# A loan of 384 columns, earlier exchanges and turns, and transfers paced by TensorE's columns

## The chip, the cores and the metric

The kernel runs on one core of a Trainium2 chip (trn2). The metric is the time of one execution on the device in microseconds (us), as the median of several runs. A core has TensorE (PE in the profile; its weight loads are PEld), VectorE (DVE), ScalarE (ACT), GpSimd (POOL) and SyncE (SP), each with its own queue of instructions, and 16 DMA engines that move data for all queues. Here almost all transfers are issued by SP.

## What is computed

Attention with a threshold over 8 batches and 8 heads of 576 rows and 64 columns, then a bilinear feed-forward layer on the heads side by side (4608 tokens of 512 numbers, 1536 inner columns), all in 32-bit floats:

```python
def _attn_ref(q, k, v, tau):
    scale = 1.0 / np.sqrt(q.shape[-1])
    scores = scale * np.matmul(q, k.transpose(0, 1, 3, 2))
    thresh = np.max(scores, axis=-1, keepdims=True) - tau
    scores = np.where(scores >= thresh, scores, -1000000000.0)
    scores = scores - np.max(scores, axis=-1, keepdims=True)
    attn = np.exp(scores)
    attn = attn / (np.sum(attn, axis=-1, keepdims=True) + 1e-09)
    return np.matmul(attn, v).astype(np.float32)

def _moe_ref(x, w_a, w_b, w_out):
    a = x @ w_a
    b = x @ w_b
    return (a * b @ w_out).astype(np.float32)
```

Between the two, `attn_out.transpose(0, 2, 1, 3)` brings the heads of a token side by side.

## The kernel before

**Units and slots.** The heads are taken in 32 pairs (`pairs`), the rows of a pair in five units: four of 128 rows and one of 64 (`NT`). The outer loop goes over 160 units; one turn of it (`g`) is a slot, and each slot works on several units at once, each at another stage:

- `scores(g)`: TensorE computes the scores of unit g into two PSUM tiles (L352), DVE takes the row maxima (L359) and the threshold (L360).
- `weigh(g)`: ACT takes the exponential (L380), DVE masks it and sums the rows (L383); then the reciprocal of the sums (L394, L396) and `normalise` on ACT (L402).
- `turn_blocks(g-1)`: DVE transposes the weights in blocks of 32 x 32 (L446), and SP writes them in four transfers to a buffer in memory, `swap` (L457).
- `turn_back(g-2)`: SP reads them from there in turned order into a tile `wT` (L466, 576 KB in one transfer; L469 for the unit of 64 rows). There are two tiles `wT`.
- `weighted(g-3)` (`PV_LAG` is 3): where a half of a pair is complete, TensorE multiplies the turned weights with v (L483, a *product*, of 128 columns, or 160 where the unit of 64 rows goes with it), and `settle` copies the result to x: one copy on ACT (L490), two on DVE (L491), and the same again into `xt` for the 32 columns of the unit of 64 rows.

The first eight units are turned by TensorE itself (`BY_PE`). In the first 30 or so slots the weights of the feed-forward layer are loaded as well, and ACT, POOL and DVE convert them.

**The feed-forward layer as filler.** When four pairs have filled a tile of x, `exchange_blocks` copies its two halves of partitions crosswise into a second tile, `xS` (POOL, eight copies, L506), makes two tiles of differences, `xU` (L513), and puts the block on a list. `ffn` is a generator that yields after every few matmuls: 128 columns a step in `sevens_of` (L633), 256 in `plain` (L706) and in the output layer (L763). A column here is one column of the moving operand in four matmuls that share TensorE's array. `advance(cols)` runs the generator until as many columns have been spent. Each slot has a budget of columns (`pace`), given out in four portions (`PORTIONS`: 0.3, 0.35, 0.15, 0.2): the first after `turn_blocks`, the second ahead of the product, the last two at the slot's end. The product's own columns are taken off the account (`running["owed"]`), so the last two portions of a slot with a product are mostly eaten by it.

**Buffers.** All results in PSUM go through four tiles of two banks each (`banks`). The tiles xT, xS, xU and xt share seven buffers (`XT_BUFS`); `make_x` runs the feed-forward layer ahead until a buffer is free. `kept` and `osb` are rows of the output that `store` sends out (L833).

**Order.** Each engine runs its instructions in the order in which the code emits them; `keep_order` fixes that. SP's queue in a slot is: swap writes of the unit before (they wait for L446), read back of the unit before that (it waits for the product that last used the `wT` tile), then loads of q, k (`load`, L147) and v (`load_v`, L170), then output. `prep` transposes a loaded q or k in place on DVE (L320). A transfer by SP uses one of eight semaphores in turn, so it waits for the eighth transfer before it.

**Start.** q and k of the first pairs come as rows (`load_rows`), TensorE transposes them (`prep_pe`, L333) and DVE copies the result (`prep_copy`, L338). Six small operations on DVE (L305 to L310) derive five numbers from `tau`, which SP loads (L290) after the first rows.

Of the kernel before, what the change touches and what calls it, by code (L numbers as in the profile page):

```python
# [14 lines left out]
ALU = mybir.AluOpType  # L15
# [7 lines left out]
PV_LAG = 3  # L23
BY_PE = 8
# [4 lines left out]
CATCH_UP = 0.05  # L29
PACE_EARLY = 0.04  # L30
ROOM = 1024
PORTIONS = (0.3, 0.35, 0.15, 0.2)
RAWS = 4
TW_BUFS = 3
# [18 lines left out]
def kernel(  # L53
# [41 lines left out]
    Q = 32  # L95
# [24 lines left out]
    loads = pool("loads", 3)  # L120
    work = pool("work", 2)
    small = pool("small", 2)
    scratch = pool("scratch", 3, space=bass.MemoryType.DRAM)
    psum = pool("psum", 4, space=PSUM)

    def banks(n, name):
# [5 lines left out]
    NPR = len(pairs)  # L132
    loaded = {}

    def load(i, name, engine=nc.sync):

        b, hp = pairs[i]
        src = {"q": q, "k": k}[name[0]]
        n0, n1 = {"k": (0, NB), "q0": (0, HALF // Q), "q1": (HALF // Q, NB)}[name]
        bufs = HP if name == "k" else Q_BUFS  # L140
        most = NB if name == "k" else NB - HALF // Q
        t = work.tile([P, most, Q], FP32, tag=name[0] + "T", bufs=bufs, name=name[0] + "T")[:, 0:n1 - n0]
        for j in range(2):
            rows = src[b, 2 * hp + j].rearrange("(e n) d -> e n d" if name == "k" else "(n e) d -> e n d", e=Q)
            for h in range(2):
                r = slice((2 * j + h) * Q, (2 * j + h + 1) * Q)
                engine.dma_start(t[r], rows[:, n0:n1, h * Q:(h + 1) * Q])  # L147
        loaded.setdefault(i, {})[name] = t

    def load_rows(i, name, room, engine=nc.sync):  # L150
# [7 lines left out]
    def load_v(i, again=False):  # L158
        b, hp = pairs[i]
        if not again:  # L160
            loaded[i]["v"] = loads.tile([P, NSLOT, D], FP32, tag="vm", bufs=HP, name="vm")
        for j in range(2):
            rows, half = v[b, 2 * hp + j], loaded[i]["v"][j * D:(j + 1) * D]
            if i >= HP or again:
                if i < HP:
                    rows = rows.rearrange("(c s p) d -> p c s d", c=2, p=Q)
                else:
                    rows = rows.rearrange("(p c s) d -> p c s d", c=2, p=Q)
                for c in range(2):
                    nc.sync.dma_start(half[c * Q:(c + 1) * Q], rows[:, c])  # L170
            else:
                nc.sync.dma_start(half, rows.rearrange("(s p) d -> p s d", p=D))

# [20 lines left out]
    for F in range(NF):  # L194
# [1 line left out]
    NPIECES = len(pieces)  # L196
    raws, stages, extra, taken = {}, {}, [], {}
    state = {"loaded": 0, "added": 0, "converted": 0, "rows": 0, "sums": False, "through": 0, "over": False,
             "layer": False, "reading": False, "first": 0}


    NSUM = NF // 2 * 3 * CH
# [82 lines left out]
    rooms = [t.rearrange("p (n w) -> p n w", n=NR) for t in rooms]  # L285
    load_rows(0, "q", rooms[0])
    load_rows(0, "k", rooms[1], nc.scalar)
    load_rows(1, "q", rooms[2])
    load_rows(1, "k", rooms[3], nc.scalar)
    nc.sync.dma_start(tau_sb, tau.to_broadcast([P, 1]))  # L290
    load_weights(2)
    load_rows(2, "q", rooms[4])
    load_rows(2, "k", rooms[5])
# [7 lines left out]

    ok, e_scale, e_nscale, cut, big = (scalars[:, c:c + 1] for c in range(5))
    nc.vector.tensor_scalar(ok, tau_sb, 0.0, None, op0=ALU.is_ge)  # L305
    nc.vector.tensor_scalar(e_scale, ok, SCALE, None, op0=ALU.mult)
    nc.vector.tensor_scalar(e_nscale, ok, -SCALE, None, op0=ALU.mult)
    nc.vector.tensor_scalar(big, ok, -BIG, BIG, op0=ALU.mult, op1=ALU.add)
    nc.vector.tensor_scalar(cut, tau_sb, 0.0, INV_SCALE, op0=ALU.max, op1=ALU.mult)
    nc.vector.tensor_tensor(cut, cut, big, op=ALU.add)  # L310


    prepared, scored, weights, turned, whole = {}, {}, {}, {}, {}
    x_of, xtail_of = {}, {}
    blocks, complete, swaps = [], [], {}

    def prep(i, name):

        mT = loaded[i].pop(name).rearrange("p n e -> p (n e)")
        nc.vector.transpose(mT, mT)  # L320
        prepared.setdefault(i, {})[name] = mT
# [119 lines left out]
    def turn_blocks(i, u):  # L441

        ws, _ = weights.pop((i, u))
        t = whole.pop((i, u))
        for w in ws:
            nc.vector.transpose(w, w)  # L446
        if u < NT:
            swap = scratch.tile([G, P, NSLOT * Q], FP32, tag="swap", name="swap")
        else:
            swap = scratch.tile([2, P, NSLOT * Q], FP32, tag="swapt", name="swap")  # L450
        swaps[i, u] = swap
        for g in range(G):
            if u < NT:
                to, n = swap[g], G
            else:
                to, n = swap[g % 2, (1 - g // 2) * D:(2 - g // 2) * D], 2
            nc.sync.dma_start(to.rearrange("(r p) e -> p r e", p=Q),  # L457
                              t[g * Q:(g + 1) * Q, 0:n * NSLOT].rearrange("p (r s) e -> p r (s e)", r=n))

    def turn_back(i, u):  # L460

        swap = swaps.pop((i, u)).rearrange("g p e -> p g e")
        if u < NT or i < HP:
            turned[i, u] = turned_tile()
            n = G if u < NT else 2
            nc.sync.dma_start(turned[i, u][:, 0:n].rearrange("p g s e -> p g (s e)"), swap)  # L466
        else:
            for y in range(2):
                nc.sync.dma_start(turned[i, 2 + y][:, G].rearrange("p s e -> p (s e)"), swap[:, y])  # L469

    def join(out, lo, hi):
        nc.scalar.copy(out, lo)
# [43 lines left out]
    def exchange_blocks():  # L516
        while complete and not state["layer"] and not blocks:
            x, what = complete.pop(0)
            xs = x_tile("xS")
            for hp in range(HP):  # L520
                exchange(x, xs, hp, 0, HALF, nc.gpsimd)
            blocks.append(((x, xs) + ((x_sums(x), x_sums(xs)) if state["first"] >= 3 * SEVENS else ()), what))

    def weighted_unit(i, u):

# [13 lines left out]
    def weighted(i, h):  # L539

        b, hp = pairs[i]
        n = width(i, h)
        if h < 2:
            groups = G + (n > HALF)
# [6 lines left out]
        if h < 2:  # L551
            if hp == 0:
                x_of[b, h] = x_tile("xT")
            settle(x_of[b, h][:, hp, :], pv, 0, P, read)
            if hp == HP - 1:
                complete.append((x_of.pop((b, h)), ("half", b, h)))
        if n % HALF:
            t = b % GT
# [271 lines left out]
    def store(n):  # L830

        for _ in range(n):
            nc.sync.dma_start(*pending.pop(0))  # L833

    BLOCK_COLS = NF * 2 * HP * HALF + 2 * NF * DM

# [1 line left out]

        return BLOCK_COLS - (NF // 2 * CH if state["sums"] else 0) - (SEVENS * 2 * HP * P if state["first"] >= 3 * SEVENS else 0)

    running = {"ffn": None, "owed": 0.0, "left": 0, "done": 0, "rest": 0, "room": 0}

    def advance(cols):
        running["owed"] += cols
        while running["owed"] > 0:
# [16 lines left out]
            if step is None:  # L862
                running["ffn"] = None
                state["through"] += 1
            else:
                running["owed"] -= step
                running["left"] -= step
                running["done"] = running["done"] + step if rest else 0
                running["rest"] = rest
                running["room"] = min(ROOM, whole // 2)  # L870
# [8 lines left out]

    def make_x(count):  # L880

        while (len([k for k in x_of if k != (0, 0)]) + len(xtail_of) + len(complete) + sum(len(x) for x, _ in blocks)
               + (state["reading"] and running["tiles"]) + count > XT_BUFS):
            owed = running["owed"]
            running["owed"] = 0.0
# [20 lines left out]
    first = {i: g for g, (i, u) in enumerate(units) if u == 0}  # L906
    second = {i: g for g, (i, u) in enumerate(units) if u == 2}

    for name in ("q", "k"):
        prep_copy(*prep_pe(0, name))  # L910
    early = {}

    def convert_rest(g, k):
# [10 lines left out]
        n += size  # L924
    for g in range(len(units) + PV_LAG):
        written = len(pending)
        state["converted"] = state["added"]
        here = g < len(units)
        converting = bool(early.get(g)) or bool(early.get(g - 1))
        if here:  # L930
            i, u = units[g]
            scores(i, u)
        exchange_blocks()
        pace = (PACE if g > BY_PE else PACE_EARLY) * BLOCK_COLS
        if g > BY_PE:
# [16 lines left out]
            turn_blocks(*units[g - 1])  # L952
        if g > BY_PE:
            advance(PORTIONS[0] * pace)
        if here:
            weigh(i, u)
        if here and g < BY_PE:
# [3 lines left out]
        if g < 3:  # L961
            prep_copy(*prep_pe(g + 1, "k"))
        for p in range(HP, NPR):
            for name, d in (("q0", 1), ("k", 2), ("q1", 1)):
                if g == (second if name == "q1" else first)[p] - d:
                    prep(p, name)
        if g > BY_PE:
            advance(PORTIONS[1] * pace)
            n = g - PV_LAG
            if BY_PE <= n < len(units) and part(*units[n]):  # L970
                p, h = part(*units[n])
                if pairs[p][1] == 0:
                    make_x(2 if h == 1 and p >= HP and pairs[p][0] % GT == 0 else 1)
                make_room()
                weighted(*part(*units[n]))
                running["owed"] -= NSLOT * width(*part(*units[n])) // 2
            if BY_PE + 1 < g <= len(units) + 1:
                turn_back(*units[g - 2])
        for n in early.get(g, [])[:1]:
            convert_first(n)  # L980
# [22 lines left out]
            load_v(g - BY_PE, again=True)  # L1003
        store(written)
        if g > BY_PE:
            advance(PORTIONS[2] * pace)
            advance(PORTIONS[3] * pace)

# [9 lines left out]
        if g > first[HP] + 1 and not converting and state["first"] < 3 * SEVENS:  # L1018
            first_sums(state["first"] % 3, state["first"] // 3)
            state["first"] += 1  # L1020
    state["over"] = True
    while complete or blocks or running["ffn"] is not None:
        advance(DM)
        store(len(pending))
# [33 lines left out]
```

## Time and profile before

| | |
|---|---|
| median of 8 runs | 1462.7 us (1459.64 to 1465.43) |
| the profiled execution, time | 1465.27 us |
| its span, first to last instruction | 1463.5 us |
| granted TensorE clock, mean | 0.993 |
| records of matmuls | 34208 |
| transfers in memory | 223.21 MB, mean 153 GB/s |

The page names groups of instructions by line, engine and the program's tiles. Its waits give the idle time of an engine just before an instruction and the instruction that ended it; "issue" stands for time for which the profile shows no cause. Of the groups that the change concerns:

| group | count | mean ns |
|---|---|---|
| L352 scores, 288 columns | 2016 + 288 records | 404, 441 |
| L483 products | 5184 records | 275 |
| L633 feed-forward, 128 columns | 14336 records | 270 |
| L446 transposes on DVE | 272 | 754 |
| L383 masking on DVE | 288 | 800 |
| L320 transposes of qT on DVE | 56 | 474 |
| L506 exchange on POOL | 152 | 400 (median) |

Records of TensorE overlap, four at a time and more, so that a mean is not the time that one takes of the span. Transfers, with size and median time from issue to landing: swap writes 480 of 144 KB, 2.6 us; wT reads 120 of 576 KB, 4.7 us, and 56 of 144 KB, 3.0 us; k 112 of 72 KB, 4.2 us; q 224 of 32 and 40 KB, 3.9 and 4.3 us; v 128 of 72 KB, 3.3 us; output 30 of 256 KB, 4.0 us.

### The profile page before, as it was taken

How to read it: one execution, taken by the hardware profiler on the slowest of the kernel's cores; microseconds unless marked ns; L12 is line 12 of the kernel's file. 1: busy time of each engine (PE TensorE's matmuls, PEld its weight loads, DVE VectorE, ACT ScalarE, POOL GpSimd, SP SyncE). 2: the span in 40 equal slices, each digit the busy share in tenths (PEclk: the TensorE clock that was granted, in tenths of full speed). 3: DMA queues.
4: the chain of work that ended last, by engine and by line, in shares of the span. 5: the costliest groups of instructions: out<-in, count | busy, mean ns of one | idle time of the engine just before them, and what ended most of it. 6: DMA issues, size and time to landing. Idle time of an engine off the chain costs nothing.

```text
span 1463.5 us, 76332 instructions
## 1 busy us (share of the span) xinstructions
PE 1390.3 (95%) x34208; PEld 1254.0 (86%) x34208; DVE 1014.5 (69%) x2245; ACT 684.5 (47%) x1243; POOL 480.9 (33%) x668
## 2 busy tenths in 40 slices
PE   5779999999999999999999999999999999999998
PEld 4678687888889989889998888888898879999998
DVE  6898688787767787586757677767867676655223
ACT  5786455545545554454444445444545455431110
POOL 2674723423060606033324224240606060605000
PEclk9999999999999999999999999999999999999999
DMA  9976677678756865576545766567756686550000
GB/s 208 227 209 181 162 180 185 169 175 194 192 134 161 186 182 148 143 174 179 144 131 135 169 168 165 129 170 163 183 146 152 160 194 160 127 150 31 4 18 17
DMA packets 325080, 223.21 MB, mean 153 GB/s; under 512 B 169616, under 2 KB 308880, under 8 KB 324752
## 3 DMA queue, kind: packets, MB, share of 16 engines
q1 hardware_dynamic: 322384, 217.73, 60.4%
q8 instruction: 269, 4.41, 1.3%
q10 hardware_dynamic: 2368, 0.59, 0.2%
q14 instruction: 59, 0.48, 0.1%
HBM read 128.58 MB, written 89.65 MB: 149 GB/s over the span
## 4 chain that ended last, share of the span: by engine, by line
PE 81%; DMA 6%; DVE 6%; SPq 3%; issue 3%; ACT 1%; POOL 1%; ACTq 0%; DVEq 0%; POOLq 0%
PE pab L633 26%; PE po L763 18%; PE pab L706 18%; PE pv L483 9%; PE sc L352 9%; DMA wT<-swap 1%; DVE mx L359 1%; DVE tw L446 1%; DMA raw<-in_moe_w_a_dram 1%; SPq L457 1%; DMA sums_u<-in_moe_w_a_dram 1%; PE po L809 1%; DVE tw L383 1%; DMA more_u<-in_moe_w_a_dram 1%; SPq L225 1%
## 5 line engine op out<-in xcount | busy, mean ns | idle before, releaser
L359 DVE TENSOR_REDUCE mx<-sc 128x1 f32<-128x576 f32 x288 | 205.7, 751 | 137.9 <-PE sc L352 134.6
L402 ACT ACTIVATE tw<-tw,rcp 128x576 f32<-128x576 f32 x272 | 198.0, 770 | 216.0 <-DVE rcp L396 216.0
L380 ACT ACTIVATE tw<-sc,bias,scalars 128x576 f32<-128x576 f32 x288 | 239.6, 832 | 9.8 <-DMA vm<-in_v_dram 0.2
L599 POOL TENSOR_TENSOR h<-h,u 128x512 f32<-128x512 f32 x28 | 35.1, 1275 | 618.1 <-DVE h L676 483.5
L383 DVE SCALAR_TENSOR_TENSOR tw<-sc,thr,tw 128x576 f32<-128x576 f32 x288 | 223.5, 800 | 14.2 <-ACT tw L380 14.0
L763 PE MATMUL po<-wo_sb,h 64*64 64x256 f32 x3264 | 223.2, 377 | 0.0
L352 PE MATMUL sc<-kT,qT 64*64 64x288 f32 x2016 | 190.8, 404 | 10.3 <-ACT xt L490 5.8
L446 DVE STREAM_TRANSPOSE tw<-tw 128x576 f32<-128x576 f32 x272 | 196.1, 754 | 0.8 <-ACT tw L402 0.8
L483 PE MATMUL pv<-wT,vm 64*64 64x160 f32 (+3 forms) x5184 | 182.0, 275 | 11.8 <-DMA wT<-swap 5.6
L763 PEld LDWEIGHTS po<-wo_sb,h 64*64 64x64 f32 x3264 | 170.0, 133 | 23.0
L483 PEld LDWEIGHTS pv<-wT,vm 64*64 64x64 f32 x5184 | 166.5, 135 | 22.0 <-issue 9.3
L763 PE MATMUL po<-sums_u,h 64*64 64x256 f32 x2448 | 164.2, 376 | 1.6 <-DVE h L714 1.6
L732 POOL TENSOR_TENSOR h<-h 128x256 f32<-128x256 f32 x168 | 117.5, 731 | 113.2 <-PE po L763 99.0
L763 PEld LDWEIGHTS po<-sums_u,h 64*64 64x64 f32 x2448 | 124.7, 133 | 19.8 <-DVE h L714 2.3
L352 PEld LDWEIGHTS sc<-kT,qT 64*64 64x64 f32 x2016 | 113.4, 133 | 32.8 <-ACT xt L490 12.2
L633 PE MATMUL pab<-xU,wb_sb 64*64 64x128 f32 x4096 | 132.9, 270 | 0.7 <-issue 0.7
L379 ACT ACTIVATE bias<-mx,scalars 128x1 f32<-128x1 f32 x288 | 83.0, 288 | 100.4 <-DVE mx L359 100.3
L633 PEld LDWEIGHTS pab<-xU,wb_sb 64*64 64x64 f32 x4096 | 127.1, 133 | 3.1 <-issue 0.9
L491 DVE COPY xT<-pv 64x128 f32<-64x128 f32 (+1 forms) x136 | 38.1, 280 | 118.6 <-PE pv L483 117.4
L633 PE MATMUL pab<-xS,wa_sb 64*64 64x128 f32 x2048 | 112.3, 270 | 3.4 <-issue 1.7
L490 ACT COPY xT<-pv 128x128 f32<-128x128 f32 (+1 forms) x68 | 17.7, 260 | 199.8 <-PE pv L483 199.7
L706 PE MATMUL pab<-xS,wb_sb 64*64 64x256 f32 (+1 forms) x1536 | 98.9, 359 | 0.0
(137 smaller groups left out, 2435.8 us busy)
## 6 DMA issues: line engine op xcount, KB each, us to landing
swap<-tw SPq DMA_DIRECT2D x480, 144.0 KB, 2.6
wT<-swap SPq DMA_DIRECT2D x120, 576.0 KB, 4.7
vm<-in_v_dram SPq DMA_DIRECT2D x128, 72.0 KB, 3.3
swap<-tw SPq DMA_DIRECT2D x128, 72.0 KB, 2.1
kT<-in_k_dram SPq DMA_DIRECT2D x112, 72.0 KB, 4.2
wT<-swap SPq DMA_DIRECT2D x56, 144.0 KB, 3.0
out_dram<-kept SPq DMA_DIRECT2D x30, 256.0 KB, 4.0
qT<-in_q_dram SPq DMA_DIRECT2D x112, 40.0 KB, 4.3
```

What stands on the lines that cost most here:

```text
L352: nc.tensor.matmul(sc[j if u < NT else 0][to, c], qT[r, q0:q0 + D], kT[r, c * SH:(c + 1) * SH], start=True, stop=True)
L359: nc.vector.tensor_reduce(mx[:, c], sc[j], axis=AX.XY, op=ALU.max)
L379: nc.scalar.activation(bias[:, j:j + 1], mx[:, j:j + 1], AF.Copy, scale=e_nscale)
L380: nc.scalar.activation(wb[j], sb[j], AF.Exp, bias=bias[:, j:j + 1], scale=e_scale)
L383: nc.vector.scalar_tensor_tensor(out=wv, in0=sb[j], scalar=thr[:, j:j + 1], in1=wv, op0=ALU.is_ge, op1=ALU.mult, accum_out=sums[:, j:j + 1])
L402: nc.scalar.activation(w, w, AF.Copy, scale=rcp[:, j:j + 1])
L446: nc.vector.transpose(w, w)
L483: nc.tensor.matmul(pv[c * D:(c + 1) * D, y], vm[rows, s], wT[y](rows, s), start=(s == 0), stop=(s == NSLOT - 1))
L633: nc.tensor.matmul(out[c * D:(c + 1) * D, r, f * P:(f + 1) * P], w[g][k][rows, w0:w0 + D], moving[k][rows], start=(fresh and k == 0 and f ...
L706: nc.tensor.matmul(pab[c * D:(c + 1) * D, r], w[rows, f // n, k, fs + c * D:fs + (c + 1) * D], moving, start=(k == 0), stop=(k == H - 1))
L732: (nc.vector if state["over"] else nc.gpsimd).tensor_tensor(*a, **kw)
L763: nc.tensor.matmul(po[c * D:(c + 1) * D, r, y], ht[rows, t0:t0 + D], other[rows, f], start=(f == 0), stop=(f == NF // 2 - 1))
```

## The change

Seven edits:

1. *A list of transfers.* Loads of q, k and v, swap writes, reads back and output go through `post`. Up to slot 40 it issues them at once. From slot 41 on it puts them on one list, `bulk`, in order. `passed(columns)` counts TensorE's columns (steps of the feed-forward layer, scores, products) and calls `pump` for each 320 (`PUMP`): it takes one post off the list and makes its first transfer wait for TensorE's instruction emitted last. `flush` empties the list up to a key that is needed now; posts older than a slot go out at a slot's start. A post is one swap write, one quarter of a read back, one quarter of k, two transfers of q or v, or one of output.
2. *The read back in pieces*: one transfer for each of the four blocks of the tile instead of one for all.
3. *Turned back sooner*: in a slot without a product, `turn_back` stands at the slot's start, ahead of the scores, and not behind the second portion. `swap` has five buffers instead of three.
4. *The loan*: in a slot with a product up to 384 columns (`held`) of the second portion are kept back and spent behind the product.
5. *x exchanged ahead*: `exchange_blocks` also copies the parts of x that are settled though the block isn't complete (`settled`, `ahead`), where no block is waiting and the first layer isn't running.
6. *q turned sooner*: `prep` of q0 and q1 stands ahead of `weigh`, that of k stays behind it.
7. *tau moved*: it is loaded by ACT's queue after pair 0's k, the six operations stand behind the first copies, and ACT makes the first copy of k.

```diff
+PUMP = 320
...
-    scratch = pool("scratch", 3, space=bass.MemoryType.DRAM)
+    scratch = pool("scratch", 5, space=bass.MemoryType.DRAM)
...
+    def post(key, *moves):
+        if not state["paced"]:
+            for move in moves:
+                nc.sync.dma_start(*move)
+        else:
+            bulk.append((key, state["slot"], moves))
+
+    def pump(count=1):
+        for _ in range(min(count, len(bulk))):
+            behind = next(x.name for x in reversed(nc.cur_bb.bb.instructions) if x.engine == mybir.EngineType.PE)
+            for n, move in enumerate(bulk.pop(0)[2]):
+                moved = nc.sync.dma_start(*move)
+                if n == 0:
+                    tc.add_manual_dep(
+                        moved.ins, behind,
+                        mybir.DependencyInfo(mybir.DependencyClass.Sync, mybir.DependencyReason.DATA),
+                        reason="pace")
+
+    def flush(*keys):
+        while any(key in keys for key, _, _ in bulk):
+            pump()
+
+    def passed(columns):
+        running["pump"] = running["pump"] + columns if bulk else 0
+        while running["pump"] >= PUMP:
+            running["pump"] -= PUMP
+            pump()
...
     load_rows(0, "k", rooms[1], nc.scalar)
+    nc.scalar.dma_start(tau_sb, tau.to_broadcast([P, 1]))
...
-    nc.sync.dma_start(tau_sb, tau.to_broadcast([P, 1]))
...
     def turn_back(i, u):
+        flush(("tw", i, u))
         swap = swaps.pop((i, u)).rearrange("g p e -> p g e")
+        key = "wT", i, min(u // 2, 1) if i >= HP else u // 2
...
-            nc.sync.dma_start(turned[i, u][:, 0:n].rearrange("p g s e -> p g (s e)"), swap)
+            for y in range(0, n, 1):
+                post(key, (turned[i, u][:, y:y + 1].rearrange("p g s e -> p g (s e)"), swap[:, y:y + 1]))
...
-            xs = x_tile("xS")
-            for hp in range(HP):
+            xs, done = ahead.pop(what[1:], (None, 0)) if what[0] == "half" else (None, 0)
+            xs = xs or x_tile("xS")
+            for hp in range(done, HP):
                 exchange(x, xs, hp, 0, HALF, nc.gpsimd)
...
+        if not state["layer"] and not blocks:
+            for key, count in settled.items():
+                xs, done = ahead.get(key) or (x_tile("xS"), 0)
+                for hp in range(done, count):
+                    exchange(x_of[key], xs, hp, 0, HALF, nc.gpsimd)
+                ahead[key] = xs, count
...
-    for name in ("q", "k"):
-        prep_copy(*prep_pe(0, name))
+    prep_copy(*prep_pe(0, "q"))
+    kT, tp = prep_pe(0, "k")
+    nc.scalar.copy(kT.rearrange("p (c k) -> p c k", c=2), tp)
...
+        state["slot"], state["paced"] = g, g > 40
+        while bulk and bulk[0][1] < g - 1:
+            pump()
...
+        back = ()
+        if BY_PE + 1 < g <= len(units) + 1:
+            n = g - PV_LAG
+            back = (1 if BY_PE <= n and part(*units[n]) else 0,)
+            if not back[0]:
+                turn_back(*units[g - 2])
         if here:
             i, u = units[g]
             scores(i, u)
+            passed(S)
...
         if g > BY_PE:
-            advance(PORTIONS[1] * pace)
             n = g - PV_LAG
+            held = 0.0
+            if BY_PE <= n < len(units) and part(*units[n]):
+                held = 384 - (PORTIONS[2] + PORTIONS[3]) * pace + NSLOT * width(*part(*units[n])) // 2
+                held = min(max(held, 0.0), 384)
+            advance(PORTIONS[1] * pace - held)
...
                 weighted(*part(*units[n]))
+                passed(NSLOT * width(*part(*units[n])) // 2)
                 running["owed"] -= NSLOT * width(*part(*units[n])) // 2
-            if BY_PE + 1 < g <= len(units) + 1:
+            if back and back[0] > 0:
                 turn_back(*units[g - 2])
...
         if g > BY_PE:
+            if held:
+                owed, running["owed"] = running["owed"], 0.0
+                advance(held)
+                running["owed"] += owed
             advance(PORTIONS[2] * pace)
             advance(PORTIONS[3] * pace)
```

## The prediction

> **What bounds the kernel now.** First the page's busy table, its rows of slices and its chain, to see which engine sets the end.
>
> ```profile
> PE 1390.3 (95%) x34208; PEld 1254.0 (86%) x34208; DVE 1014.5 (69%) x2245; ACT 684.5 (47%) x1243; POOL 480.9 (33%) x668
> ...
> PE   5779999999999999999999999999999999999998
> ...
> DMA  9976677678756865576545766567756686550000
> ...
> PE 81%; DMA 6%; DVE 6%; SPq 3%; issue 3%; ACT 1%; POOL 1%; ACTq 0%; DVEq 0%; POOLq 0%
> ```
>
> TensorE (PE) is busy for 95% of the span and makes 81% of the chain. The change takes no matmul away, so it can only win from the 1463.5 - 1390.3 = 73.2 us in which PE is idle, and from time in which its clock is low. The next view is the list of PE's waits, longest first in total: total, number, longest.
>
> ```profile
> PE sc L352 <- DVE kT L338: 9.4, 4, 3.7
> PE sc L352 <- ACT xt L490: 5.8, 5, 1.2
> PE pv L483 <- DMA wT<-swap: 5.6, 3, 2.4
> ...
> PE pv L483 <- issue: 3.7, 3, 2.3
> ...
> PE sc L352 <- DVE xt L491: 3.1, 3, 1.1
> ...
> PE pv L483 <- PE pab L706: 1.9, 2, 1.0
> ...
> PE pab L633 <- POOL xS L506: 1.5, 2, 0.7
> ...
> PE sc L352 <- ACT xT L490: 0.7, 1, 0.7
> ```
>
> The first row belongs to the first 35 us. The others are what the change touches: scores that wait until a product's result is copied out (xT, xt), products that wait for turned weights (wT), feed-forward steps that wait for an exchange (xS). The chain of waits around the longest wT wait (start, duration, what) shows how it arises:
>
> ```profile
> 250.24 0.75 DVE tw L446
> ...
> 251.00 0.31 SPq L457
> ...
> 253.17 0.43 SPq L457
> ...
> 254.01 4.02 DMA wT<-swap
> ...
> 258.07 3.42 PE pv L483 x67
> ```
>
> The read back (L466) is queued behind the four swap writes of the next unit (L457), and these wait for DVE's transposes (L446). So the read leaves only at 254.01, lands 4.02 us later, and PE stands. What follows is in the table of windows (PE busy, PEld, DVE, ACT, POOL, granted clock, DMA share, GB/s), at both long waits:
>
> ```profile
> 258.62:262.04 3.42, 3.42 (x73) 3.42 (x67) 0.90 (x3) 0.26 (x1) 3.10 (x7) 0.50 0.72 174
> ...
> 835.48:838.89 3.41, 3.41 (x60) 3.33 (x56) 0.00 (x0) 0.00 (x0) 0.00 (x0) 0.50 0.70 169
> ```
>
> For 3.4 us after the waits of 2.43 and 2.06 us the granted clock is 0.50: a second cost of 1.7 us for each, which the table of waits doesn't hold.
>
> **The change part by part.** The profiled execution took 1465.3 us (its span 1463.5 and 1.8 us around it), 2.6 us above the median of 1462.7; differences are taken from the profile and subtracted from the median.
>
> *The loan.* 128 feed-forward columns are four matmuls of the program, eight records (the page counts 34208 records for the program's 17128 matmuls: two for each but the 48 transposes of L333). The dense end runs 376 records of L633 in 10.47 us: 27.8 ns each, 0.22 us for a step. 384 columns are thus 0.67 us, or 0.86 us where the steps are L763's 256 columns (0.43 us each). In the built program before, all 160-column products from the middle on are followed by the next scores with no step between; afterwards by 0.67 to 0.86 us of steps, except two with 0.22 and 0.45. The scores' waits for the copies are 5.8 + 3.1 + 0.7 = 9.6 us in 9 places, 1.07 us each; 0.67 us of cover leaves 0.4. That is -6.0 us. Ends: -9.6 (all of it) and +2 (the product starts 0.67 us sooner, and three products that already waited for wT wait that much longer). I take -6, since the copies' length doesn't change.
>
> *The sooner turn back.* Where the slot has no product, `turn_back` now stands ahead of the slot's scores, so ahead of the swap writes that held it in the chain shown; it costs no instruction, and what it passes on SP's queue are those writes, whose data are read one slot later. The three waits of 5.6 us should go, and with the two longest the low clock, 2 x 1.7 = 3.4 us: -9.0. Ends: 0, and -14.6 if the other two pv rows (3.7 and 1.9) are transfers too. I take -9, as the chain names the cause. Next to end late there is the copy after the product, the row of the loan.
>
> [...]
>
> *x exchanged ahead.* The eight POOL copies of a block (L506, median 0.40 us) now run as heads settle and not all when the block is complete: POOL does the same copies, sooner. -1.5 us, the PE row; ends 0 and -4.5 (PEld's row for the same wait, of which most is covered). `make_x` now counts the early xS against seven buffers, so feed-forward steps are sometimes run sooner; they are charged to the same account, and PE has the same work. 0.
>
> *tau, first copies.* Before, DVE's first instruction waits for tau until 8.82, does six small operations, then two copies of 0.75 us, and the first scores start at 10.92. Now tau is on ACT's queue, the six stand after the copies, and ACT copies k beside DVE: the transposes end at 7.22, plus about 0.75, so scores at about 8.1, 2.8 us sooner. But the chain from 26.53 to 75.3 us is made of weight transfers, and the DMA row reads 9 in the first two slices. These move only by the issue of tau that SP loses, 0.35 us. -0.4; ends 0 and -2.8.
>
> *q turned sooner.* 56 transposes of qT (0.47 us) go ahead of the masking (L383) on DVE. The masking, and what follows it to the next slot's swap write, is later by 0.47 us in those slots; hidden as DVE is busy 69% and PE's rows for L383 are under 3 us in all. 0; without that cover 56 x 0.47 = 26 us.
>
> *The list.* From slot 41 on each transfer stands behind a PE instruction, one post for every 320 columns (0.56 us). A wT read is now four of 144 KB: the program has 544 wT reads where it had 180, and 1162 semaphore waits on SP where it had 384. At 0.38 us an issue (row wT<-swap of SP) that is 364 x 0.38 = 138 us on SP, under 1 us a slot, on a queue that is not in PE's way. What matters is the last quarter: in the built program it is released 5.5 us of PE work before its product in the tightest of 47 products, 9.7 in the median. Landing is 4.6 us for 576 KB and 3.0 for 144 KB. 0 us, hidden by that slack; the price without it is the second rival.
>
> [...] The swap writes here are issued four in 1.75 us and land in 2.6 each, so they overlap.
>
> *PE's own waits.* More transfers mean more semaphores: 241 more semaphore instructions on PE, mostly ahead of products. The row nearest: 107 such waits stood before products, median 51 ns, and PE's idle "issue" before products is 3.7 us in 3 places, 35 ns each over the 107; so 0 to 241 x 0.035 = 8.4 us. As 104 of 107 show no idle, +3.
>
> Sum: -6.0 - 9.0 - 1.5 - 0.4 + 3.0 = -13.9; 1462.7 - 13.9 = 1448.8 us (a profiled one like the last: 1451.4).
>
> **The rivals.**
> 1. *The gain is larger*: all the rows named, at their far ends, and no cost: -9.6 - 14.6 - 4.5 - 2.8 = -31.5, 1431 us. For it: PEld's rows show more waits that almost reach PE. Against: the issue rows name no transfer, and the start is held by the weights.
> 2. *Turned weights come late, slower*: the list is in order, so a read stands behind q, k, v and output transfers, and behind swap writes that still wait for DVE; release is not issue. Place: pv. With slacks as built, a delivery (release to landing) of 7 us costs 4.7 us over the 47 products, 8 us 12.7, 9 us 24.5. The other parts give -6.0 - 1.5 - 0.4 + 3.0 = -4.9, so it decides from about 7 us on; at 9 us the time is 1462.7 - 4.9 + 24.5 = 1482 us. For it: SP waited 320 us for DVE's transposes before. Against: 3.0 us landings leave 2.5 us even in the tightest product.
> 3. *No change that can be told*: a wait removed comes back at the next eviction. PE's busy state needs DVE and ACT to return banks, which the change doesn't hasten; PEld's issue waits before L633 (12.8 us) stay or grow by what is won, but for the clock: 1462.7 - 3.4 + 2 = 1461. Against: DVE has 31% idle.
>
> **How the numbers follow.** Forecast 0.60, with its own range 1438 to 1459 (the loan and the turn back at half and at nearly full ends); larger gain 0.12; no change 0.10; late weights 0.18. 0.2%, about 3 us, is what a measurement of this kernel can tell from no change: faster is 0.60 + 0.12 = 0.72, same 0.10, slower 0.18. The range 1436 to 1466 holds the forecast, the no-change case, half of the larger gain and a fifth of the late weights: 0.2 is left out, most of it above.
>
> **What would show it.** Right: PE's waits for wT gone and no clock of 0.50 between 200 and 1400 us; scores' waits for xt, xT at 4 us or less; the first scores near 8.1 us; PE's idle time near 60 us. Wrong: pv rows with transfers above 10 us (late weights); idle "issue" before pv above 8 us (PE's waits); waits of L633 and L763 for DVE and ACT grown by 8 us or more (the stall only moved); L383 named by PE above 5 us (q).

## The result, and the profile after

The changed kernel takes 1455.2 us in the median of 22 runs (1447.98 to 1462.73), the kernel before, in all the runs made beside it, 1463.5 (62 runs, 1456.62 to 1472.17). The ratio is 0.9939, its 95% interval 0.9926 to 0.9953: by the ratio 8.9 us less (6.9 to 10.8), where the prediction had 13.9. The profiled execution took 1458.28 us, its span 1456.5. Single runs of one kernel differ by some 7 us either way, so rows of one profile are read for where the time goes, and the medians for how much.

The page of the changed kernel, the same rows as before the change (busy time by engine, TensorE and DMA in 40 slices, the chain's shares):

```profile
PE 1391.2 (96%) x34208; PEld 1261.3 (87%) x34208; DVE 1018.0 (70%) x2244; ACT 684.8 (47%) x1244; POOL 482.4 (33%) x668
...
PE   6789999999999989999999999999999899999998
...
DMA  9976677666756676566645676466755676450000
...
PE 85%; DMA 5%; DVE 3%; SPq 3%; issue 2%; ACT 1%; DVEq 0%; ACTq 0%
```

TensorE's busy time is what it was; its idle time is 1456.5 - 1391.2 = 65.3 us, where it was 73.2. So the whole gain is idle time. TensorE's waits (total us, times, longest) show which:

```profile
PE pv L513 <- DMA wT<-swap: 18.3, 10, 3.4
PE sc L379 <- issue: 5.9, 7, 3.6
PE pab L746 <- issue: 5.6, 3, 2.5
...
PE sc L379 <- DVE tw L410: 3.8, 6, 1.4
PE pv L513 <- issue: 3.1, 3, 1.6
...
PE pab L673 <- issue: 0.3, 1, 0.3
```

(L379 are the scores, L513 the products, L673 and L746 the feed-forward steps, L410 the masking; before, L352, L483, L633, L706 and L383.) Three things happened. The scores' waits for xt and xT, 9.6 us in 9 places, are gone. The products' wait for turned weights, which was to go, is three times as long: 18.3 us in 10 places, where it was 5.6 in 3. And a row that the prediction did not look at has gone: steps of L633 that waited for "issue" are 0.3 us in one place, where the trace before has

```profile
PE pab L633 <- issue: 7.8, 12, 1.9
```

(Two other "issue" rows have grown, those of the scores and of L746, from 0.5 and 2.0 us to 5.9 and 5.6; 9.2 of these 11.5 us lie in the first 120 us, among the first heads.)

Part of the gain is older than the list: slot 41, with which the list begins, starts at 330.6 us in the trace before and at 326.0 in this one (by its first row maximum on DVE). So 4.6 of the 7.0 us between the two spans are won before it, and only 2.4 behind.

One of the longest waits for turned weights shows how it comes about. The timeline of the changed kernel (start, length, engine and line, what, and in brackets the idle time before):

```profile
816.99 2.29 SPq L151 DMA_DIRECT2D wT<-swap  x3
...
819.37 1.79 SPq L151 DMA_DIRECT2D swap<-tw  x4
...
821.26 3.89 SPq L151 DMA_DIRECT2D kT<-in_k_dram  x4
...
825.25 1.21 SPq L151 DMA_DIRECT2D out_dram<-kept  x2
...
826.55 1.03 SPq L151 DMA_DIRECT2D wT<-swap  x2
...
829.01 4.43 PE L513 MATMUL pv<-wT,vm 64*64 64x160 f32 x66 [2.78 <-DMA wT<-swap]
```

The two pieces of the read that the product waits for stand behind four loads of k and two of output, which were posted before it and are held to TensorE's columns. The chain of waits in the same stretch has the steps one after another (start, length, what):

```profile
824.57 0.58 SPq L151
...
825.91 0.55 SPq L151
...
826.55 2.32 DMA wT<-swap
...
829.01 0.45 PE pv L513 x2
```

SP is released by TensorE at 824.5, then issues what was held up, and only then the read. And the low clock is still there (windows: length, busy time of PE, PEld, DVE, ACT, POOL, granted clock, DMA share, GB/s):

```profile
830.18:833.59 3.41, 3.41 (x59) 3.41 (x55) 0.00 (x0) 0.00 (x0) 0.00 (x0) 0.50 0.52 117
338.66:342.07 3.41, 3.41 (x60) 3.41 (x55) 0.04 (x1) 0.00 (x0) 1.41 (x2) 0.50 0.54 131
1161.27:1164.68 3.41, 3.41 (x60) 3.41 (x56) 0.97 (x1) 0.00 (x0) 2.36 (x2) 0.50 0.57 130
```

Three windows after late reads, where the kernel before had two. So the gain isn't the one that was forecast.

### The profile page after: what moved, and what is told of

It is laid out like the page before. It is cut to its first block, busy times and chain, and to the rows that moved or that the text cites. A ratio compares the mean times of both kernels' runs of the same rounds, so it can differ in the third digit from the quotient of the medians.

```text
span 1456.5 us, 77671 instructions
## 1 busy us (share of the span) xinstructions
PE 1391.2 (96%) x34208; PEld 1261.3 (87%) x34208; DVE 1018.0 (70%) x2244; ACT 684.8 (47%) x1244; POOL 482.4 (33%) x668
## 4 chain that ended last, share of the span: by engine, by line
PE 85%; DMA 5%; DVE 3%; SPq 3%; issue 2%; ACT 1%; DVEq 0%; ACTq 0%
PE pab L673 26%; PE po L803 19%; PE pab L746 18%; PE sc L379 10%; PE pv L513 10%; DMA wT<-swap 3%; SPq L142 1%; PE po L849 1%; DMA vm<-in_v_dram 1%; DVE mx L386 1%; SPq L190 1%; DMA raw<-in_moe_w_a_dram 1%; DVE tw L473 1%; DMA sums_u<-in_moe_w_b_dram 1%; SPq L259 1%
## 5 line engine op out<-in xcount | busy, mean ns | idle before, releaser
L407 ACT ACTIVATE tw<-sc,bias,scalars 128x576 f32<-128x576 f32 x288 | 239.6, 832 | 11.7 <-PE pab L673 1.6
L410 DVE SCALAR_TENSOR_TENSOR tw<-sc,thr,tw 128x576 f32<-128x576 f32 x288 | 222.9, 799 | 9.6 <-ACT tw L407 8.2
L803 PE MATMUL po<-wo_sb,h 64*64 64x256 f32 x3264 | 229.4, 377 | 0.0
L513 PE MATMUL pv<-wT,vm 64*64 64x160 f32 (+3 forms) x5184 | 190.2, 280 | 23.4 <-DMA wT<-swap 18.3
L513 PEld LDWEIGHTS pv<-wT,vm 64*64 64x64 f32 x5184 | 172.3, 138 | 39.6 <-issue 21.6
L379 PE MATMUL sc<-kT,qT 64*64 64x288 f32 x2016 | 197.6, 405 | 3.8 <-issue 2.3
L803 PE MATMUL po<-sums_u,h 64*64 64x256 f32 x2448 | 169.1, 376 | 0.3 <-DVE h L754 0.3
L379 PEld LDWEIGHTS sc<-kT,qT 64*64 64x64 f32 x2016 | 116.0, 133 | 31.6 <-issue 6.5
L673 PE MATMUL pab<-xU,wb_sb 64*64 64x128 f32 x4096 | 138.0, 269 | 0.0
L673 PEld LDWEIGHTS pab<-xU,wb_sb 64*64 64x64 f32 x4096 | 130.8, 133 | 1.8
L673 PE MATMUL pab<-xS,wa_sb 64*64 64x128 f32 x2048 | 111.4, 269 | 0.0
L746 PE MATMUL pab<-xS,wb_sb 64*64 64x256 f32 (+1 forms) x1536 | 101.7, 359 | 2.1 <-issue 2.1
```

Of the source, the lines that this page charges most:

```text
L379: nc.tensor.matmul(sc[j if u < NT else 0][to, c], qT[r, q0:q0 + D], kT[r, c * SH:(c + 1) * SH], start=True, stop=True)
L407: nc.scalar.activation(wb[j], sb[j], AF.Exp, bias=bias[:, j:j + 1], scale=e_scale)
L410: nc.vector.scalar_tensor_tensor(out=wv, in0=sb[j], scalar=thr[:, j:j + 1], in1=wv, op0=ALU.is_ge, op1=ALU.mult, accum_out=sums[:, j:j + 1])
L513: nc.tensor.matmul(pv[c * D:(c + 1) * D, y], vm[rows, s], wT[y](rows, s), start=(s == 0), stop=(s == NSLOT - 1))
L673: nc.tensor.matmul(out[c * D:(c + 1) * D, r, f * P:(f + 1) * P], w[g][k][rows, w0:w0 + D], moving[k][rows], start=(fresh and k == 0 and f ...
L746: nc.tensor.matmul(pab[c * D:(c + 1) * D, r], w[rows, f // n, k, fs + c * D:fs + (c + 1) * D], moving, start=(k == 0), stop=(k == H - 1))
```

## The experiments

Twelve runs. The table has the median, the ratio to the kernel before in the runs made beside it (its medians there lie between 1462.2 and 1466.9), with its interval, and two rows of TensorE's waits in the one profiled execution (us in times): products for turned weights, and 128-column feed-forward steps for "issue".

| kernel | median us | ratio | interval | wait for wT | issue, ffn |
|---|---|---|---|---|---|
| before | 1463.5 | 1 | | 5.6 in 3 | 7.8 in 12 |
| after | 1455.2 | 0.9939 | 0.9926-0.9953 | 18.3 in 10 | 0.3 in 1 |
| e1, after without the list | 1444.3 | 0.9879 | 0.9856-0.9903 | 12.3 in 8 | 1.8 in 2 |
| e2, after, reads first in the list | 1454.1 | 0.9943 | 0.9918-0.9968 | 8.2 in 5 | 1.2 in 2 |
| e3, before + loan | 1467.6 | 1.0015 | 0.9995-1.0036 | 9.4 in 7 | 6.4 in 13 |
| e4, after without loan | 1458.3 | 0.9967 | 0.9946-0.9988 | 9.1 in 6 | 1.2 in 4 |
| f1, e1 with reads of 576 KB | 1455.8 | 0.9954 | 0.9936-0.9973 | none | 15.1 in 17 |
| f2, after with reads of 576 KB | 1462.3 | 0.9985 | 0.9965-1.0005 | 0.6 in 1 | 17.5 in 16 |
| f3, before + sooner turn back | 1464.4 | 1.0021 | 1.0001-1.0041 | none | 17.6 in 15 |
| f4, before + loan + sooner | 1460.5 | 0.9986 | 0.9968-1.0004 | 0.6 in 1 | 11.9 in 14 |
| g1, before + pieces | 1477.1 | 1.0080 | 1.0051-1.0109 | 15.3 in 10 | 2.3 in 5 |
| g4, before + pieces + sooner | 1457.5 | 0.9941 | 0.9920-0.9962 | 7.4 in 6 | 1.8 in 4 |
| g2, e1, loads first | 1444.0 | 0.9857 | 0.9830-0.9885 | 9.5 in 7 | 1.2 in 4 |
| g3, g2 with reads of 288 KB | 1445.7 | 0.9874 | 0.9846-0.9903 | none | 11.7 in 14 |

### The list

e1 issues every transfer at once, as the kernel before does; all else is the change.

```diff
-        state["slot"], state["paced"] = g, g > 40
+        state["slot"], state["paced"] = g, False
```

> The changed kernel without the list: every transfer is issued at once, as up to slot 41, all else as changed. In the changed kernel products waited 18.3 us for wT in 10 places (before: 5.6 in 3), with three windows at half clock behind them. Theory: the list is what makes the reads late (they stand behind k, output and swap writes that wait for DVE). Then the pv row for wT falls below 6 us, PE's idle time from 65 to about 53 us, the clock windows of 2 x 1.7 us go, and the ratio to the kernel before is about 0.984 (0.981 to 0.988). Rival: the reads are late because they are split and stand elsewhere, the list has no part; then the row stays near 18 us and the ratio near 0.994. A third: without the pace the transfers collide more, ratio above 0.997.

1444.25 us, 0.9879: the list costs 0.6%, some 9 us, and without it the kernel is faster than both. The wait for turned weights falls from 18.3 to 12.3 us, not below 6: the list makes a third of it.

e2 keeps the list and puts the pieces of a read at its head.

```diff
-            bulk.append((key, state["slot"], moves))
+            at = sum(1 for _ in itertools.takewhile(lambda x: x[0][0] == "wT", bulk)) if key[0] == "wT" else len(bulk)
+            bulk.insert(at, (key, state["slot"], moves))
```

> The changed kernel with one edit in the list: a piece of a read back is put ahead of all posts of other kinds, behind earlier pieces. Theory (late because of what stands ahead of it in the list): the pv row for wT falls from 18.3 us to under 6, ratio about 0.984 to 0.988. Rival (the pace itself, one post for 320 columns, or the pieces make it late): the row stays above 12 us, ratio 0.992 to 0.996.

The row falls to 8.2 us in 5, so the order in the list does make reads late. But the median, 1454.07, is that of the changed kernel. (Its profile, with a span of 1447.1, is of one of its quicker runs.) So it is not shown that the late reads are the whole price of the list; the rest stays open.

### The loan

e3 is the loan alone in the kernel before, e4 the changed kernel without it.

```diff
-            advance(PORTIONS[1] * pace)
+            advance(PORTIONS[1] * pace - held)
...
+            if held:
+                owed, running["owed"] = running["owed"], 0.0
+                advance(held)
+                running["owed"] += owed
```

> The kernel before with the loan alone. Prediction's term: -6.0 us, the scores' rows for xt and xT from 9.6 to about 4 us. The changed kernel's rows show no such wait on PE, so theory: -6 to -10 us, ratio 0.993 to 0.996, with wT rows unchanged or up to 2 us longer. Rival: the loan gives back at the product what it wins at the scores: ratio 0.998 to 1.001, the wT row 5 us or more above 5.6.

```diff
-                held = min(max(held, 0.0), 384)
+                held = 0.0
```

> The changed kernel without the loan (nothing kept back of the second portion). If the loan is worth the prediction's 6 us here too, the ratio rises from 0.994 to 0.998 (0.996 to 1.000), with 8 us or more of scores' waits for xt and xT. Rival: without it the product comes 0.67 to 0.86 us later, which the late reads need; the wT row falls by 5 us or more and the ratio stays at 0.993 to 0.996.

The rows xt and xT disappear in e3, as they should, and the time does not: 1.0015. What is won there is lost at other places, first of all at the next product (waits of e3; before, the same rows had 5.6, 3.7 and 0.5 us):

```profile
PE pv L483 <- DMA wT<-swap: 9.4, 7, 2.9
...
PE pv L483 <- issue: 5.0, 5, 3.3
PE sc L352 <- issue: 4.7, 10, 0.7
```

In e4 the scores wait for the copies again:

```profile
PE sc L379 <- ACT xt L520: 6.8, 6, 1.2
...
PE sc L379 <- DVE xt L521: 1.9, 2, 1.0
```

e4 is 0.0028 above the changed kernel, 4 us, but the intervals overlap. The loan is worth nothing alone, and perhaps 4 us among the other edits, which these runs do not show clear of noise.

### The sooner turn back, and the size of a read

f3 is edit 3 alone in the kernel before, f4 with the loan; f1 and f2 put the read back into one transfer, without and with the list.

```diff
+            if not back[0]:
+                turn_back(*units[g - 2])
         if here:
             i, u = units[g]
             scores(i, u)
```

> The kernel before with the sooner turn back alone (reads in one piece, no list, five swap buffers). Prediction's term: the three waits for wT (5.6 us) and two half-clock windows (3.4 us) go, -9 us, ratio 0.994 (0.991 to 0.996). Rival: SP's queue holds the read anyway (behind loads of k issued in the slot before), a wait of about the same size stays: ratio 0.998 to 1.002, wT row 4 us or more.

> The kernel before with the loan and the sooner turn back, nothing else. The loan alone gave 1.0015 [0.9995, 1.0036], as its product comes 0.67 us sooner and its wT row went from 5.6 to 9.4 us. Theory: the loan pays only where the reads come sooner, the two together -10 to -15 us: ratio 0.990 to 0.993, scores' rows for xt and xT under 2 us, wT row under 7. Rival: the two simply add, ratio as for the sooner turn back alone within 0.002.

```diff
-            for y in range(0, n, 1):
-                post(key, (turned[i, u][:, y:y + 1].rearrange("p g s e -> p g (s e)"), swap[:, y:y + 1]))
+            post(key, (turned[i, u][:, 0:n].rearrange("p g s e -> p g (s e)"), swap))
```

> The changed kernel without the list, and with each read back in one transfer as before. Without the list alone the ratio was 0.988 [0.986, 0.990], with 12.3 us of wT waits left in 8 places: there the read of the unit of 64 rows is issued behind four pieces of an earlier read (2.71 us on SP), four swap writes and four loads of k (2.60 us). Theory (the pieces fill SP's queue, and PE's extra semaphore waits cost some): wT row under 8 us, ratio 0.983 to 0.987. Rival (smaller pieces land sooner, 3.0 against 4.6 us, which outweighs the queue): wT row above 14 us, ratio 0.989 to 0.993.

> The changed kernel, list and all, with each read back in one transfer: 364 transfers fewer on the list, which is one post for 320 columns. Theory (the list's length makes reads late): wT row from 18.3 to under 10 us, ratio 0.987 to 0.991. Rival (order and pace, not length): row 14 us or more, ratio 0.993 to 0.997.

f3 does to the named row what was forecast: no product waits for turned weights. The time does not fall: 1.0021, where the step's -9.0 us would be 0.9938. f4 gives 0.9986, 0.0035 below f3: the loan is worth some 5 us here, again with overlapping intervals, and neither expectation holds (the two together at 0.990 to 0.993, or the loan adding nothing). f1 and f2 have no wait for turned weights, or 0.6 us of it, as the theory wanted, and are yet slower than e1 and than the changed kernel, by 0.0075 and 0.0046, and above every range that was forecast for them. So the named wait is gone in these kernels, or nearly, and the time is not. The longest row of TensorE's waits is now this one in f3, and in f1 it is the same:

```profile
PE pab L633 <- issue: 17.6, 15, 2.3
```

```profile
PE pab L672 <- issue: 15.1, 17, 2.5
```

These are steps in the middle of the feed-forward layer, and the profile names nothing that they wait for. What is it? One of the long waits of f1, in its timeline, first SP and then TensorE:

```profile
426.50 0.37 SPq L142 DMA_DIRECT2D wT<-swap  x1
```

```profile
431.91 0.41 PE L672 MATMUL pab<-xU,first_u 64*64 64x128 f32 x5
433.54 0.66 PE L672 MATMUL pab<-xU,first_u 64*64 64x128 f32 x16 [1.21 <-issue]
```

A read is issued at 426.50 (reads of this size land after 4.8 us in f1's median), and TensorE stops at 432.3. The page's list of DMA queues has two of a kind that no line of the kernel fills, "instruction". The larger is (queue and kind, packets, MB, share of the 16 engines):

```profile
q8 instruction: 269, 4.41, 1.2%
```

That is 16.4 KB a packet. The trace before has 269 packets in q8 as well, and of TensorE 34208 matmuls, 34208 weight loads, 478 semaphore instructions and 3 drains: 68897 records, 256.1 for each packet. The changed kernel has 270 packets and, with 719 semaphore instructions, 69138 records: 256.1 again. So q8 is taken to be TensorE's own instructions, 256 to a packet, an estimate from these counts. A packet then feeds 128 matmuls, 3.6 us of dense 128-column steps at 27.8 ns. The six longest delays of such steps in f1 (from the start of the matmul before to the start of this one, less 27.8 ns), and the packets ahead of them, in us:

```
TensorE resumes   delay     q8 packet          since the packet before   from issue of the last wT read to the packet
 433.54            1.46      431.00 -  432.08   6.84                      4.50
 508.39            1.56      506.16 -  507.16   6.27                      6.19
 589.69            1.43      587.39 -  588.45   6.44                      3.68
 836.16            1.44      833.59 -  834.71   7.35                      4.01
1276.48            1.76     1274.07 - 1275.00   7.48                      3.47
1301.81            2.71     1299.15 - 1300.22   6.28                      4.23
```

Each time TensorE goes on 1.2 to 1.6 us after the end of a packet that came 6.3 to 7.5 us after the one before it; half of all packets come within 4.9 us. In five of the six cases a read of 576 KB had been issued 3.5 to 4.5 us before the packet started and landed 0.8 to 3.5 us after that start; in the sixth it had landed.

That TensorE waits for the packet itself is a reading that counting supports. Take as late each 128-column matmul that starts over 0.25 us too late behind another one, between 330 and 1330 us: f1 has 19, late by 18.7 us in all. Count TensorE's instructions up to each (matmuls, weight loads and its semaphore instructions) in blocks of 256, and the packets. All 19 stand at the same place of a block, to within one instruction, and the number of the block less that of the packet that ended last is the same each time: this is read as the late matmul being of the block that has just come. The same holds for all 18 late ones of f2 (20.4 us), 20 of 31 in f3 (23.4 us) and 20 of 31 in the kernel before (13.3 us); the changed kernel has 3 at that place (1.1 us), e1 2 (2.0 us). Of f1's 19, 16 had a read in flight when the packet started, though one was in flight at only 88 of the 194 packets.

### Pieces alone, pieces and sooner, other sizes

If large reads hold back TensorE's instructions, splitting them, which the prediction had costed as nothing but SP's time, should be the edit that wins.

```diff
-            nc.sync.dma_start(turned[i, u][:, 0:n].rearrange("p g s e -> p g (s e)"), swap)
+            for y in range(n):
+                nc.sync.dma_start(turned[i, u][:, y:y + 1].rearrange("p g s e -> p g (s e)"), swap[:, y:y + 1])
```

> The kernel before with one edit: each read back of the turned weights goes in four transfers of 144 KB, not in one of 576 KB. Theory (large reads in flight hold back the blocks of TensorE's own instruction stream): the issue row of L633, 7.8 us in 12 before, falls below 2 us; the wT row (5.6 us) may grow by 2 to 4 as SP has more to issue; time about 1455 us, ratio 0.993 to 0.997. Rival (the size of the reads is not the cause; the four pieces only did well together with the other edits): the issue row stays at 6 us or more, ratio 0.998 to 1.002.

Half of it came true: the issue row falls to 2.3 us. The waits of g1:

```profile
PE pv L484 <- DMA wT<-swap: 15.3, 10, 4.5
...
PE pv L484 <- issue: 4.6, 3, 3.6
...
PE pab L634 <- issue: 2.3, 5, 0.9
```

Five late steps at a block's place are left (3.5 us by the count above, 13.3 before), but the reads, four issues each and still behind the slot's swap writes, are later: products wait 9.7 us longer for turned weights, and the median is worse, 1.0080. Neither theory had forecast a loss. So the two edits were put together.

> The kernel before with two edits: reads back in four pieces of 144 KB, and the sooner turn back. Alone, the pieces measured 1.008 (issue row of L633 down from 7.8 to 2.3 us, wT row up from 5.6 to 15.3), and the sooner turn back 1.002 (no wT row, issue row up to 17.6). Theory (each edit cures the wait that the other makes: the pieces the instruction stream's, the earlier place the reads'): together the issue row stays below 4 us and the wT row falls below 8 us; ratio 0.990 to 0.996, below both. Rival (the pieces cost time on SP that the earlier place does not give back, and the gain without the list came from the other edits): the wT row stays at 10 us or more and the ratio is 1.002 to 1.010.

```profile
PE pv L484 <- DMA wT<-swap: 7.4, 6, 1.8
...
PE pab L634 <- issue: 1.8, 4, 0.8
```

| | read behind the swap writes | sooner turn back |
|---|---|---|
| one read of 576 KB | 1 | 1.0021 |
| four of 144 KB | 1.0080 | 0.9941 |

Each edit alone loses or does nothing; together they win 8.6 us. The sooner turn back is worth +3 us with large reads and -20 with small ones (from 1.0080 to 0.9941). This theory holds, in its rows and in its range: each cures the wait that the other makes.

g2 and g3 go on from e1. In g2 the loads of q, k and v stand ahead of the slot's swap writes, so that the next read does not stand behind loads of k; g3 has reads in two transfers.

```diff
+        if g > 40:
+            loads_of()
         if g > BY_PE and g <= len(units):
             turn_blocks(*units[g - 1])
```

> The changed kernel without the list, and from slot 41 on the loads of q, k and v stand on SP's queue ahead of the slot's swap writes, not at the slot's end, where they come just ahead of the next sooner read back. Theory (the late reads stand behind loads of k issued at the end of the slot before): the wT row, 12.3 us without the list, falls below 5 us and the time to 1438 to 1443 us, ratio 0.982 to 0.986. Rival (what is late is the swap writes, which wait for VectorE's transposes, so that the loads in front do not matter): the wT row stays at 9 us or more, ratio 0.987 to 0.990.

```diff
-            for y in range(0, n, 1):
+            for y in range(0, n, 2):
```

> The run before it with reads in two transfers of 288 KB. Theory (the delay of the instruction stream grows with the size of the read in flight): the issue rows of L672 and its like lie between those of 144 KB (about 2 us) and of 576 KB (15 us), at 4 to 9 us, and the ratio is 0.003 to 0.005 above that of four pieces. Rival (a threshold below 576 KB, or the number of issues on SP that counts): issue rows below 3 us and a ratio equal to or below that of four pieces.

g2 has the lowest median of all, 1443.96, but its interval overlaps that of e1. Its ratio, 0.9857, lies in the theory's range, with an interval that reaches into the rival's; the wT row only falls from 12.3 to 9.5, the rival's side. So the loads are not the main reason for late reads; SP still waits 107.3 us for DVE's transposes there. In g3 no product waits for weights, and the other wait is back:

```profile
PE pab L673 <- issue: 11.7, 14, 1.7
```

That is more than the theory's 4 to 9 us: 288 KB acts nearly like 576 KB (15.1 us in f1), and 144 KB hardly at all (1.2 us in g2). By the count above g3 has 17 late steps, all at a block's place (15.4 us), g2 4 there (1.7 us). The ratio, 0.9874, can't be told from g2's: the one wait has come in place of the other.

## Why the prediction was right, and where it was wrong

The sign and the range held. The sum did not: its largest term comes about only together with an edit that was costed at nothing, and another edit costed at nothing is a loss of the same size. That the sum came within 5 us of the measured gain is in good part luck.

*The sooner turn back, -9.0.* This step failed. Alone the edit measured +3 us (0.1 to 6). The rows were read rightly: the wait named is gone in f3. The error was "Next to end late there is the copy after the product": next to be late were, by the count above, TensorE's instructions: 23.4 us at a block's place in f3, where it was 13.3. Why the same large reads cost more there when they start sooner is not shown. The row stood in the waits before (L633 for issue, 7.8 us in 12, the second longest), was left out of the lines quoted, and rival 3 set the issue waits of L633 down as a place that a gain might move to, without asking what they wait for.

*The split of the reads, "138 us on SP ... a queue that is not in PE's way".* This is the other half of the same error. The split takes 5.5 us from the issue row of L633 (7.8 to 2.3 us in g1) and, alone, makes the reads late enough to lose 12 us. Together with the sooner turn back it gives the -8.6 us that the prediction had for the turn back alone: about the right number for another reason, which is luck. With everything else equal, 144 KB gives 0.9879 (e1) and 576 KB 0.9954 (f1).

*The list, 0.* Mis-sized: about +9 us. Here the second rival was the right one, in place and mechanism ("stands behind q, k, v and output transfers ... release is not issue"), and its sign for "pv rows with transfers above 10 us" came up at 18.3, though 12.3 of that stand without the list too. The measured price lies between those it gave for deliveries of 7 us (4.7) and 8 us (12.7), not at the 24.5 of 9 us; and the other parts won more than the -4.9 it was set against, so the sign of the whole stayed. The slack of 5.5 us was counted from the release of the last quarter; the transfers released with it take SP 0.6 us each before it.

*PE's own waits, +3.* Not seen in the one trace: idle issue before products is 3.1 us, where it was 3.7.

*The loan, -6.* Its rows went further than forecast (9.6 us to 0, where 3.6 were to stay), and it is too large in the sum: 0 alone, some -4 or -5 among the others, not clear of noise.

*x ahead -1.5, tau -0.4, q 0.* Not tried one by one. The POOL row for xS is gone, and the first scores start at 7.91 us (8.1 was forecast). The prediction left only 0.4 us of that start in the sum, as weight transfers were to hold what follows; but slot 41 starts 4.6 us sooner, and which of the edits does that is not shown. For q, "under 3 us in all" was misread: the waits for the masking (L383) before the scores were 2.6 us, with the other rows 4.6. They are 5.8 now (3.8 before the scores), above the bound of 5 that was to speak against q, but by only 1.2 us more than before. From g4 to e1 these three and the loan make 0.9941 to 0.9879, some 9 us with an uncertainty of about 5, where the prediction had 7.9 for them.

So by the runs: -8.6 for pieces and turn back, about -9 for the loan and the small edits, about +9 for the list; these three lie on one line of kernels (before, g4, e1, after), so that their sum is the measured one by construction; each is good to 3 to 5 us, and in another order the terms would come out otherwise.

*The clock.* Windows of half clock, 3.4 us each, stood behind two long waits before (2.43 and 2.06 us) and stand behind three after, of 3.41, 2.78 and 2.02 us. Between 200 and 1400 us f3 and g3, in which no product waits for weights, have no such window. The length of the wait alone doesn't decide: no window follows the wait of 2.31 us at 514 us in the changed kernel, nor that of 2.47 us at 1301.8 in f1, while one follows the 2.02 us.

## What to carry to other kernels

When an engine shows short idle times with no releaser in the middle of independent work, look whether its instructions arrive late, and what large transfer was in flight, before a term is added up for the waits that do have names. Two edits on one queue can each lose alone and win together, so the size of a transfer and its place in the queue are best tried as a pair. A list that holds transfers back to an engine's progress keeps them in order too: what is needed next must not be posted behind what can wait.

## What was not expected of the hardware

While the kernel before runs, a DMA queue that the page calls "instruction" (q8) moves 4.41 MB in 269 packets, one for each 256.1 of TensorE's records. By the count above TensorE stands at a block's place for 13.3 us in that kernel, 18.7, 20.4 and 23.4 us in f1, f2 and f3, and 1.1, 2.0, 3.5 and 1.7 us in the changed kernel, e1, g1 and g2, which read 144 KB at a time; that it waits there for a late packet is the reading given above. That splitting the read decides is shown by five pairs which differ in nothing else, in the row of 128-column steps that wait for "issue" (before and g1 7.8 and 2.3 us, f3 and g4 17.6 and 1.8, f1 and e1 15.1 and 1.8, f2 and after 17.5 and 0.3, g3 and g2 11.7 and 1.2); whether it is the size of a transfer or that the pieces are issued one after another, they don't separate. How a read delays a packet is not shown: the records give the packets' times, not what they queue behind. Still open are also the part of the list's cost that e2 does not explain, and why 288 KB is nearly as bad as 576 KB.
